# Another order of the head's stages, and q and k of nine head pairs in 2 KB rows

## The chip, the cores and the metric

The kernel runs on one core of one Trainium2 chip. The metric is the device time of one execution in microseconds (us), and the figure of a kernel is the median of its runs. One further execution of the kernel before was taken with the profiler; the profile and the trace are of that execution.

## The reference

Two attentions are computed over the same q, k and v (8 batches, 8 heads, 576 tokens, 64 values a head), and their sum goes through a gated feed-forward network.

```python
q_d, k_d, v_d = (t.reshape(B, H, 144, 4, D).mean(axis=3) for t in (q, k, v))
out_up = np.repeat(sm_attn(q_d, k_d, v_d), 4, axis=2)        # pooled: softmax over 144 means
mask = np.abs(pos[:, None] - pos[None, :]) < 4               # local: a band of 7 keys
out_local = softmax(where(mask, scale * q @ k.T, -1e9)) @ v
x = (out_up + out_local).transpose(0, 2, 1, 3).reshape(4608, 512)
out = (np.maximum(x @ w_gate, 0) * (x @ w_val)) @ w_out      # 512 -> 1536 -> 512
```

## The kernel before

The work comes in 32 pairs of heads. A pair is one round, `s`; four pairs make a batch. The instructions of each engine run in the order in which the program issues them; that order is written out by hand, and no scheduler changes it.

A round does the following for its pair. `load_qk` and `load_v` fetch q, k and v into the staging tiles `qst`, `kst` (four buffers each) and `vst` (three) by DMAs that SP issues. `cast_q`, `cast_k` (two halves, c = 0 and 1) and `cast_v` turn them into 16-bit tiles `qk16` and `vw`. For the first nine pairs (`N_PE = 9`) `turn_pe` transposes q and k on TensorE into `qkT` and sums groups of four tokens into `pd` with further matmuls; from pair 9 on `turn_dma` transposes by DMA and `pool_q` and `pool_k` make the sums on GpSimd.

`pooled_v` averages v; `scores` makes the scores of both attentions in the PSUM tile `at`, which all rounds share. The pooled branch is `pooled_max`, `pooled_exp` (two heads, four activations in all), `pooled_weights` (division by the sums) and `turn_pooled`, a DMA transpose that SP issues, or `turn_pooled_pe`, the same on TensorE. The local branch is `local_max`, `local_sub`, `local_exp`, `local_sum`, `local_weights` and `turn_local`, a transpose on VectorE. Two rounds later `pooled_out` and `local_out` make the two outputs, `evict_od` copies the pooled one out of PSUM, and `add_x` writes the sum into `xT`, the input of the network. `evict_vd` copies the averaged v out.

The network runs in units. A unit `h` makes 128 of the 1536 hidden values for 512 tokens: eight 128x512 matmuls (`h_ps`, L480), a relu on ScalarE (L489) and a product on VectorE (L490). A unit `y` makes 128 rows of the output in twelve matmuls (L495). There are 108 units `h` and 36 units `y`; `ffn(n)` issues the next n. The first 512 tokens are all of batch 0, so the first unit needs `add_x` of pairs 0 to 3.

The head is the code ahead of the loop over s = 4 to 33. It runs rounds 0 to 3 without units, then the outputs of pairs 2 and 3:

```python
for s in range(4):
    scores(s); pooled_v(s)
    if s >= 2:
        outputs(s - 2); evict_od(s - 2)
    cast_q(s + 1, "act"); cast_k(s + 1, 1, "pool")
    ...
    pooled_weights(s, True)        # four tensor_scalar on VectorE
    ...
    turn_local(s)
for p in (2, 3):
    outputs(p); evict_od(p); add_x(p)
```

In the loop a round issues up to four units (`early`: three in round 4, two in rounds 5 to 7, one in round 8, four from round 9 on). The weights are loaded by GpSimd's queue: `wg` and `wv` in six pieces of 256 columns each, three in the head and three in rounds 4 to 6, and `wo` in twelve pieces.

SP has one queue for all loads, the DMA transposes and the stores of the output. Its instructions go in order, so one that waits holds up those behind it.

In the kernel before, q of a pair is fetched as 96 x 12 rows of 256 B (token t in column t / 96 of partition t % 96), and k in 80 x 4 rows of 1 KB, four tokens each, with an overlap for the band's edges.

Of the kernel before, what the change touches and what calls it, by code (L numbers as in the profile page):

```python
# [16 lines left out]
N_PE = 9  # L17
# [3 lines left out]
def _np_constants():  # L21

    p = np.arange(128)
    g, i = p // 32, p % 32
    j = np.arange(32)
    diff = (j[None, :] - 4) - i[:, None]
    inside = np.abs(diff) <= 3
    mask = np.zeros((128, 6, 32), np.float32)
    for n in range(6):
        key = 24 * (4 * n + g)[:, None] - 4 + j[None, :]  # L30
        ok = inside & (key >= 0) & (key < 576)
        mask[:, n, :] = np.where(ok, 0.0, NEG)
    mask[i >= 24] = 0.0

    p32 = np.zeros((128, 32), np.float16)
    own = (i >= 4) & (i < 28)
    p32[p[own], (6 * g + (i - 4) // 4)[own]] = 0.25

    eye = np.zeros((96, 192), np.float16)
    eye[:, :96] = np.eye(96)  # L40
    eye[1:73, 96:168] = np.eye(72)
    eye[np.arange(96), 168 + np.arange(96) // 4] = 1.0
    return mask, p32, eye
# [17 lines left out]
def kernel(  # L61
# [39 lines left out]
    qst = many(4, [96, 2, 6, 64], FP32, "qst")  # L101
    kst = many(4, [96, 2, 2, 256], FP32, "kst")
# [3 lines left out]
    qk16 = many(2, [96, 14, 128], FP16, "qk16")  # L106
# [5 lines left out]
    eye = pool.tile([96, 192], FP16, name="eyec")  # L112
# [20 lines left out]
    def load_qk(p):  # L133
        base = 2 * p * S * D
        nc.sync.dma_start(qst[p % 4], _dap(q, base, [[D, 96], [S * D, 2], [96 * D, 6], [1, D]]))

        st = kst[p % 4].rearrange("p h c e -> p (h c) e")
        base -= 256
        a, z = (1 if p == 0 else 0), (3 if p == NP - 1 else 4)
        nc.sync.dma_start(  # L140
            st[0:80, a:z, :],
            _dap(k, base + 72 * 256 * a, [[256, 80], [72 * 256, z - a], [1, 256]]),
        )
        if p == 0:
            nc.sync.dma_start(st[1:81, 0, :], _dap(k, base + 256, [[256, 80], [1, 256]]))
        if p == NP - 1:
            for lo, n in ((0, 64), (57, 16)):
                nc.sync.dma_start(
                    st[lo : lo + n, 3, :],
                    _dap(k, base + (216 + lo) * 256, [[256, n], [1, 256]]),  # L150
                )
# [42 lines left out]
    def cast_q(p, eng):  # L194
        copy(
            eng,
            qk16[p % 2][:, 0:6, :].rearrange("p j (h d) -> p j h d", d=D),
            qst[p % 4].rearrange("p h j d -> p j h d"),
        )

    def cast_k(p, c, eng):
        copy(
            eng,
            qk16[p % 2][0:74, 6 + 4 * c : 10 + 4 * c, :].rearrange("p r (h d) -> p r h d", d=D),
            kst[p % 4][0:74, :, c, :].rearrange("p h (r d) -> p r h d", d=D),
        )
# [8 lines left out]
    def turn_pe(p):  # L215
        x16, xt, pdt = qk16[p % 2], qkT[p % 3], pd[p % 3]
        tq = fpsum.tile([128, 6, 96], FP16, name="tq_ps", tag="f")
        for j in range(6):
            nc.tensor.transpose(tq[:, j, :], x16[:, j, :], eye[:, 0:96])
        nc.scalar.copy(out=xt[:, 0:6, :], in_=tq)  # L220
        tk = fpsum.tile([128, 8, 80], FP16, name="tk_ps", tag="f")
        for j in range(8):
            nc.tensor.transpose(tk[:, j, :], x16[0:80, 6 + j, :], eye[0:80, 0:80])
        nc.vector.tensor_copy(out=xt[:, 6:14, 0:80], in_=tk)
        pq = fpsum.tile([128, 2 * SD], FP32, name="pool_ps", tag="f")
        for j in range(6):
            nc.tensor.matmul(
                out=pq[:, 24 * j : 24 * j + 24],
                lhsT=x16[:, j, :],
                rhs=eye[:, 168:192],  # L230
                start=True,
                stop=True,
            )
        for c in range(2):
            for r in range(4):
                nc.tensor.matmul(
                    out=pq[:, SD + 72 * c : SD + 72 * c + 72],
                    lhsT=x16[0:80, 6 + 4 * c + r, :],
                    rhs=eye[0:80, 96:168],
                    start=(r == 0),  # L240
                    stop=(r == 3),
                )
        nc.scalar.copy(out=pdt.rearrange("p t g -> p (t g)"), in_=pq)

    def turn_dma(p):
        nc.sync.dma_start(
            qkT[p % 3], qk16[p % 2].rearrange("p j f -> p (j f)"), transpose=True
        )
# [55 lines left out]
    def scores(p):  # L304
        qt = qkT[p % 3].rearrange("p j t -> p (j t)")
        kt, pdt = k_view(qkT[p % 3]), pd[p % 3]
        for c in range(2):
            for h in range(2):
                lo = 64 * h
                nc.tensor.matmul(  # L310
                    out=at[0:72, h, SCO + SD * c : SCO + SD * c + SD],
                    lhsT=pdt[lo : lo + 64, 0, 72 * c : 72 * c + 72],
                    rhs=pdt[lo : lo + 64, 1, :],
                    start=True,
                    stop=True,
                    tile_position=(lo, 0),
                )
        for n in range(6):
            for g in range(4):
                c, m = n // 3, 4 * (n % 3) + g  # L320
                for h in range(2):
                    lo = 64 * h
                    nc.tensor.matmul(  # L323
                        out=at[32 * g : 32 * g + 32, 2 + h, SCO + 32 * n : SCO + 32 * n + 32],
                        lhsT=qt[lo : lo + 64, 96 * n + 24 * g : 96 * n + 24 * g + 32],
                        rhs=kt[lo : lo + 64, c, :, 6 * m : 6 * m + 8].rearrange("p r g -> p g r"),
                        start=True,
                        stop=True,
                        tile_position=(lo, 32 * g),
                    )  # L330
# [73 lines left out]
    def pooled_weights(p, apart):  # L404
        c = col[p % 2]
        nc.vector.reciprocal(out=c[0:72, 48:52], in_=c[0:72, 44:48])
        if not apart:
            ed = e_d[p % 2][0:72].rearrange("p h c n j -> p (h c) n j")[:, :, 0:6, 0:24]
            nc.gpsimd.tensor_tensor(  # L409
                out=ed, in0=ed, in1=_sap(c, (0, 72), 48, [[1, 4], [0, 6], [0, 24]]), op=ALU.mult  # L410
            )
            return
        for hc in range(4):
            ed = e_d[p % 2][0:72, hc // 2, hc % 2, 0:6, 0:24]
            nc.vector.tensor_scalar(
                out=ed, in0=ed, scalar1=c[0:72, 48 + hc : 49 + hc], scalar2=None, op0=ALU.mult
            )
# [8 lines left out]
    def turn_pooled_pe(p):  # L426
        tp = fpsum.tile([128, 8, 72], FP16, name="ad_ps", tag="f")
        ed = e_d[p % 2].rearrange("p h c (k n) j -> p (h c k) (n j)", k=2)
        for j in range(8):
            nc.tensor.transpose(tp[:, j, :], ed[0:72, j, :], eye[0:72, 0:72])  # L430
# [107 lines left out]
    nc.vector.memset(kst[0][0:32, 0, 0, :], 0.0)  # L538
    nc.vector.memset(vst[0][0:32, 0, 0, :], 0.0)
    load_qk(0)  # L540
    load_qk(1)
    load_v(0)
    load_qk(2)
    load_v(1)
    load_qk(3)
    load_v(2)
    for t in qk16:
        nc.gpsimd.memset(t[64:96, 6:14, :], 0.0)
# [4 lines left out]


    def piece(i):
        load_w(moe_w_gate, wg, 256 * i, 256 * i + 256)
        load_w(moe_w_val, wv, 256 * i, 256 * i + 256)
# [4 lines left out]

    cast_q(0, "act")
# [3 lines left out]
    turn_pe(0)  # L567
    for s in range(4):
        scores(s)
        pooled_v(s)  # L570
        if s >= 2:
            outputs(s - 2)
            evict_od(s - 2)
        cast_q(s + 1, "act")
        cast_k(s + 1, 1, "pool")
        evict_vd(s, 0)
        pooled_max(s)
        pooled_exp(s, 0)
        cast_k(s + 1, 0, "dve")
        local_max(s)  # L580
        local_sub(s)
        turn_pe(s + 1)
        pooled_exp(s, 1)
        local_exp(s)
        evict_vd(s, 1)
        cast_v(s + 1, "pool")
        pooled_weights(s, True)
        if s < 2:
            turn_pooled(s)
        local_sum(s)  # L590
        local_weights(s)
        if s >= 2:
            add_x(s - 2)
            turn_pooled_pe(s)
        turn_local(s)
        if s == 0:
            load_v(3)
            load_qk(4)
        elif s == 1:
            load_v(4)  # L600
        else:
            load_qk(s + 3)
            piece(s - 2)
            load_v(s + 3)
    for p in (2, 3):
        outputs(p)
        evict_od(p)
        add_x(p)
    piece(2)
    cast_q(5, "act")  # L610
    cast_k(5, 0, "dve")
    cast_k(5, 1, "act")

    def weights(s, part):
        if s < 7 and part in (0, 2):
            src, dst = (moe_w_gate, wg) if part == 0 else (moe_w_val, wv)
            load_w(src, dst, 256 * (s - 1), 256 * s)
# [3 lines left out]
    early = {4: (1, 1, 1, 0), 5: (1, 1, 0, 0), 6: (1, 1, 0, 0), 7: (1, 1, 0, 0), 8: (1, 0, 0, 0)}  # L621
    for s in range(4, NP + 2):
# [37 lines left out]
        if now:  # L660
            local_exp(s)
            evict_vd(s, 1)
            pooled_weights(s, False)
# [10 lines left out]
        if nxt and s + 1 < N_PE:  # L674
            turn_pe(s + 1)
# [38 lines left out]
```

## Time and profile before

| | |
|---|---|
| runs | 406.16 us median of 3 (404.42 to 406.97) |
| profiled execution | 406.47 us, of which 404.7 us from the first to the last instruction (the span) |
| TensorE busy | 360.9 us, 89% of the span |
| VectorE, ScalarE, GpSimd busy | 222.5, 213.0 and 185.3 us |
| DMA packets | 164,887, of which 142,173 under 512 B; 60.47 MB |
| mean granted TensorE clock | 0.979 of full speed |

How to read it: PE is TensorE, PEld its weight loads, DVE VectorE, ACT ScalarE, POOL GpSimd, and SP SyncE; a q behind the name is the engine's queue. L323 is line 323 of the kernel before. In the view by slices each digit is the busy share of a fortieth of the span in tenths, 9 for 90% or more; PEclk is the granted clock in the same way, and DMA the mean busy share of 16 DMA engines. In the groups of instructions a row has line, engine, operation, what it writes and reads, shapes and count, then the busy time in all and the mean ns of one, then the idle time ahead of them and what ended it. The chain of waits is followed back from the last instruction, at each step to what released it.

A view by DMA window counts the packets that start in the window by size, cumulatively.

### The profile page before, as it was taken

The numbers are of one execution on the slowest core, as the hardware profiler recorded it, in microseconds if no ns is written. First come the engines' busy times: TensorE is split into PE (matmuls) and PEld (weight loads), VectorE is DVE, ScalarE is ACT, GpSimd is POOL, SyncE is SP. The second block draws the span as 40 slices with busy tenths as digits, with TensorE's granted clock in tenths as the row PEclk, the third lists the DMA queues.
The fourth block names the chain that finished last, engine by engine and source line by source line (L and its number), as shares of the span: only waits on it lengthen the run. The fifth ranks groups of instructions, "written<-read, shape, count | busy, mean of one in ns | idle before, by whom it ended". The sixth has DMA issues, their size and how long they took to land.

```text
span 404.7 us, 12822 instructions
## 1 busy us (share of the span) xinstructions
PE 360.9 (89%) x5276; PEld 183.3 (45%) x5276; DVE 222.5 (55%) x456; ACT 213.0 (53%) x608; POOL 185.3 (46%) x256
## 2 busy tenths in 40 slices
PE   2444499768989999999999999999999999999996
PEld 2333354434444444455554444444444444444442
DVE  1465667757566666666666666666656332222210
ACT  3444567655566665665566666666654332332321
POOL 4334655657766666666555556666574000000000
PEclk9999998966999999999999999999999999999999
DMA  9989999999999999989999999999731200100112
GB/s 176 201 157 201 205 117 223 181 207 175 205 212 184 199 207 188 190 182 200 192 183 189 182 210 194 192 184 163 144 79 47 67 28 26 52 28 26 43 44 96
DMA packets 164887, 60.47 MB, mean 149 GB/s; under 512 B 142173, under 2 KB 160221, under 8 KB 164829
## 3 DMA queue, kind: packets, MB, share of 16 engines
q1 hardware_dynamic: 156364, 54.79, 71.9%
q0 software_dynamic: 8064, 4.72, 9.0%
q8 instruction: 41, 0.67, 0.7%
q10 hardware_dynamic: 400, 0.14, 0.2%
q14 instruction: 18, 0.14, 0.1%
HBM read 42.08 MB, written 9.44 MB: 127 GB/s over the span
## 4 chain that ended last, share of the span: by engine, by line
PE 77%; DVE 4%; ACT 3%; DMA 2%; POOL 2%; issue 2%; POOLq 0%; DVEq 0%; ACTq 0%
PE h_ps L480 43%; PE y_ps L495 23%; PE at L336 4%; PE at L323 3%; DMA qkT<-qk 2%; PE at L310 2%; PE at L279 1%; PE at L294 1%; DVE xT L462 1%; DVE col L349 1%; ACT e_d L383 1%; ACT r L489 1%; DVE gT L490 0%; ACT qkT L220 0%; ACT qk L188 0%
## 5 line engine op out<-in xcount | busy, mean ns | idle before, releaser
L490 DVE TENSOR_TENSOR gT<-r,h_ps 128x512 f16<-128x512 f16 x108 | 73.1, 677 | 80.3 <-PE h_ps L480 60.8
L480 PE MATMUL h_ps<-xT,wv 128*128 128x512 f16 x432 | 114.2, 387 | 1.9 <-issue 1.4
L480 PE MATMUL h_ps<-xT,wg 128*128 128x512 f16 x432 | 114.8, 389 | 0.0
L495 PE MATMUL y_ps<-wo,gT 128*128 128x512 f16 x432 | 98.5, 379 | 1.0 <-ACT r L489 1.0
L489 ACT ACTIVATE r<-h_ps 128x512 f16<-128x512 f32 x108 | 64.4, 596 | 46.7 <-PE h_ps L480 46.7
L371 POOL TENSOR_TENSOR dd<-sm,col 128x384 f32<-128x384 f32 x32 | 26.6, 830 | 104.3 <-DVE col L368 104.3
L480 PEld LDWEIGHTS <-wv 128*128 128x128 f16 x432 | 43.1, 100 | 55.7 <-issue 6.8
L495 PEld LDWEIGHTS <-gT 128*128 128x128 f16 x432 | 42.3, 98 | 52.1 <-issue 1.3
L480 PEld LDWEIGHTS <-wg 128*128 128x128 f16 x432 | 40.5, 99 | 46.6 <-issue 3.6
L383 ACT ACTIVATE e_d<-at,col 72x144 f16<-72x144 f32 x128 | 46.5, 370 | 14.3 <-DVE sm L362 9.0
L349 DVE TENSOR_REDUCE col<-at 72x4 f32<-72x576 f32 x32 | 24.0, 750 | 33.7 <-ACT vd L397 33.7
L504 ACT COPY y_sb<-y_ps 128x512 f32<-128x512 f32 x36 | 20.9, 581 | 38.7 <-PE y_ps L495 38.7
L455 ACT CAST odx<-at 128x144 f16<-128x144 f32 x32 | 8.9, 278 | 59.1 <-PE at L336 58.1
L449 DVE STREAM_TRANSPOSE pT<-pp 128x384 f16<-128x384 f16 x32 | 18.5, 578 | 34.0 <-POOL pp L441 34.0
L409 POOL TENSOR_TENSOR e_d<-e_d,col 72x576 f16<-72x576 f16 x28 | 32.0, 1143 | 3.6 <-DMA qst<-in_q_dram 1.2
L192 POOL CAST vw<-vst 128x768 f16<-128x768 f32 x32 | 26.4, 824 | 6.7 <-DMA vst<-in_v_dram 6.7
L441 POOL TENSOR_TENSOR pp<-ee,col 128x384 f16<-128x384 f16 x32 | 26.5, 827 | 5.7 <-DVE col L438 5.7
L188 ACT CAST qk<-qst 96x768 f16<-96x768 f32 x32 | 26.7, 836 | 1.3 <-DMA qst<-in_q_dram 1.3
L462 DVE TENSOR_TENSOR xT<-at,odx 128x576 f16<-128x576 f32 x32 | 23.7, 742 | 2.6 <-ACT odx L455 1.8
L383 ACT ACTIVATION_READ_ACCUMULATOR e_d<-at,col 72x1 f32 x128 | 25.0, 196 | 0.0
L190 DVE CAST qk<-kst 74x512 f16<-74x512 f32 x33 | 20.2, 614 | 5.9 <-DMA kst<-in_k_dram 5.9
L252 POOL TENSOR_TENSOR ptq<-qkT 128x288 f32<-128x288 f16 x23 | 18.7, 814 | 3.1 <-DMA qkT<-qk 3.1
(52 smaller groups left out, 355.8 us busy)
## 6 DMA issues: line engine op xcount, KB each, us to landing
vst<-in_v_dram SPq DMA_DIRECT2D x126, 96.0 KB
kst<-in_k_dram SPq DMA_DIRECT2D x30, 320.0 KB
qst<-in_q_dram SPq DMA_DIRECT2D x32, 288.0 KB
out_dram<-y_sb SPq DMA_DIRECT2D x36, 256.0 KB
wg<-in_moe_w_gate_dram POOLq DMA_DIRECT2D x6, 256.0 KB, 5.9
wv<-in_moe_w_val_dram POOLq DMA_DIRECT2D x6, 256.0 KB, 6.2
wo<-in_moe_w_out_dram POOLq DMA_DIRECT2D x12, 128.0 KB, 6.1
kst<-in_k_dram SPq DMA_DIRECT2D x2, 240.0 KB
```

The lines of the kernel that those rows point to most:

```text
L188: nc.scalar.copy(out=out, in_=in_)
L192: nc.gpsimd.tensor_copy(out=out, in_=in_)
L349: nc.vector.tensor_reduce(out=c[0:72, 36:40].rearrange("p (h c) -> p h c", h=2), in_=at[0:72, 0:2, SCO : SCO + 2 * SD].rearrange("p h (c j ...
L371: nc.gpsimd.tensor_tensor(out=dd[p % 2], in0=sm[p % 2], in1=_sap(col[p % 2], (0, 128), 0, [[1, 12], [0, 32]]), op=ALU.subtract,)
L383: nc.scalar.activation(out=e_d[p % 2][0:72, h, cc, 0:6, 0:24], in_=at[0:72, h, lo : lo + SD].rearrange("p (n j) -> p n j", j=24), func=AF.Exp,
L409: nc.gpsimd.tensor_tensor(out=ed, in0=ed, in1=_sap(c, (0, 72), 48, [[1, 4], [0, 6], [0, 24]]), op=ALU.mult)
L441: nc.gpsimd.tensor_tensor(out=pp[p % 2], in0=ee[p % 2], in1=_sap(col[p % 2], (0, 128), 24, [[1, 12], [0, 32]]), op=ALU.mult,)
L462: nc.vector.tensor_tensor(out=xT[:, kk, b * S : (b + 1) * S].rearrange("p (n g m f) -> p g n m f", n=6, g=4, f=4), in0=at[:, :, U : U + SD ...
L480: nc.tensor.matmul(out=ps, lhsT=w[:, kk, 128 * j : 128 * j + 128], rhs=xT[:, kk, TCH * c : TCH * c + TCH], start=(kk == 0), stop=(kk == 3),)
L489: nc.scalar.activation(out=r, in_=h1, func=AF.Relu)
L490: nc.vector.tensor_tensor(out=gT[c % 2][:, j, :], in0=r, in1=h2, op=ALU.mult)
L495: nc.tensor.matmul(out=ps, lhsT=gT[c % 2][:, j, 128 * t : 128 * t + 128], rhs=wo[:, j, :], start=(j == 0), stop=(j == NJ - 1),)
```

## The change

The head has five rounds instead of four. In them:

- the order in a round is `pooled_v`, `pooled_out` of two rounds before, `scores`, `local_out`; `turn_local(s - 1)` comes behind `local_max(s)`;
- the casts are two pairs ahead of the round instead of one;
- `turn_pe` only issues the matmuls; the three copies out of PSUM are functions of their own (`evict_q`, `evict_k`, `evict_pooled`) with a place of their own in the order;
- `pooled_weights` is always the one instruction on GpSimd;
- the transpose of the pooled weights of pairs 0 and 1 by DMA is issued at the start of the next round, and that of pairs 2 and 3 on TensorE in the next round;
- the outputs of pair 3 come in round 4, and three units and the two transposes of pair 4 follow the last round;
- `wg` and `wv` come in pieces of 256, 256, 512 columns in the head, and 512 in round 5.

For the first nine pairs q and k are both loaded as 80 partitions x 2 heads x 512 values: a row of 2 KB holds eight tokens. Partition i of the first 72 holds tokens 8i to 8i + 7. `turn_pe` makes 8 + 8 transposes of 72 columns and 16 pooling matmuls of 72 columns (before: 6 of 96, 8 of 80, 6 of 24 and 8 of 72). The copies write every eighth column of `qkT` (`evict_q`, `evict_k`) and every second of `pd`.

The diff, cut to its core:

```diff
 def load_qk(p):
     base = 2 * p * S * D
+    if p < N_PE:
+        for src, dst in ((q, qst), (k, kst)):
+            nc.sync.dma_start(
+                dst[p % 4][0:80, :].rearrange("p (h e) -> p h e", h=2),
+                _dap(src, base, [[512, 80], [S * D, 2], [1, 512]]),
+            )
+        return
...
 def turn_pe(p):
+    x16 = qk16[p % 2][0:72]
...
     for j in range(8):
+        nc.tensor.transpose(tq[:, j, :], x16[:, j, :], eye)
+    for j in range(8):
+        nc.tensor.transpose(tk[:, j, :], x16[:, 8 + j, :], eye)
+    pq = fpsum.tile([128, 4, 72], FP32, name="pool_ps", tag="f")
+    for a in range(4):
+        for f in range(4):
             nc.tensor.matmul(
+                out=pq[:, a, :], lhsT=x16[:, 4 * a + f, :], rhs=eye,
+                start=(f == 0), stop=(f == 3),
+            )
+    return tq, tk, pq
+
+def evict_q(p, ps):
+    nc.scalar.copy(out=flat(p)[:, 0:S].rearrange("p (i u) -> p u i", u=8), in_=ps[0])
+
+def evict_k(p, ps):
+    nc.vector.tensor_copy(
+        out=flat(p)[:, S + 4 : 2 * S + 4].rearrange("p (i u) -> p u i", u=8), in_=ps[1]
+    )
+
+def evict_pooled(p, ps):
+    nc.scalar.copy(
+        out=pd[p % 3].rearrange("p t (i a) -> p t a i", a=2),
+        in_=ps[2].rearrange("p (t a) i -> p t a i", t=2),
+    )
...
-    for s in range(4):
+    for s in range(5):
+        if s in (1, 2):
+            turn_pooled(s - 1)
+        if s < 3:
+            load_v(s + 3)
+            load_qk(s + 4)
+        pooled_v(s)
+        if s >= 2:
+            pooled_out(s - 2)
+        scores(s)
+        if s >= 2:
+            local_out(s - 2)
+            evict_od(s - 2)
+        cast_v(s + 1, "pool")
+        evict_vd(s, 0)
+        pooled_max(s)
+        local_max(s)
+        local_sub(s)
+        if s >= 1:
+            turn_local(s - 1)
+        ps = turn_pe(s + 1)
+        evict_q(s + 1, ps)
+        pooled_exp(s, 0)
+        pooled_exp(s, 1)
+        evict_vd(s, 1)
+        evict_k(s + 1, ps)
+        evict_pooled(s + 1, ps)
+        if s >= 3:
+            turn_pooled_pe(s - 1)
+        cast_k(s + 2, 0, "dve")
+        cast_k(s + 2, 1, "pool")
+        pooled_weights(s)
+        if s >= 2:
+            add_x(s - 2)
+        if s == 4:
+            outputs(3)
+            evict_od(3)
+            add_x(3)
+        local_exp(s)
+        local_sum(s)
+        local_weights(s)
+        cast_q(s + 2, "act")
+        if s >= 3:
+            load_v(s + 3)
+        if s == 3:
+            load_qk(7)
+        if 1 <= s < 3:
+            piece(256 * (s - 1), 256 * s)
+        elif s == 3:
+            piece(512, 1024)
+    ffn(3)
+    turn_local(4)
+    turn_pooled(4)
```

## The prediction

> **What bounds the kernel now.** I read the page's slices first, then the chain of waits, then the rows by form of 26 to 46 us, then the DMA windows.
>
> ```profile
> PE   2444499768989999999999999999999999999996
> DVE  1465667757566666666666666666656332222210
> PEclk9999998966999999999999999999999999999999
> DMA  9989999999999999989999999999731200100112
> ```
>
> A slice is 10.1 us. From the eleventh on TensorE is full: there the chain of work holds h_ps and y_ps matmuls alone, and a round of four units repeats every 9.49 us. Nothing in the change reaches that stretch, so its worth is how much earlier the stretch begins. In the first five slices PE is half idle, and DMA is full.
>
> The chain of waits, in order of time (start, us, what), one head round and the outputs behind it:
>
> ```profile
> 39.09 0.76 DVE col L349
> 40.43 0.71 PE tk_ps L223 x8
> 42.12 0.84 ACT e_d L383 x4
> 43.19 1.25 DVE e_d L415 x4
> 44.43 0.47 DVE col L437
> 45.16 0.62 DVE xT L462
> 46.25 0.56 PE at L336 x40
> 47.14 0.77 DVE xT L462
> 49.28 0.77 DVE xT L462
> 51.39 4.87 PE h_ps L480 x16
> ```
>
> Short pieces on three engines hand over to each other; no piece waits for a load. In the timeline scores (L310) start at 9.51, 18.18, 25.61 and 35.78 us, the outputs of pair 2 at 45.82, the first h_ps at 51.32, pooled_v of round 5 at 58.95. A round with outputs takes 10.17 and 10.04 us.
>
> The durations, from the rows by form of 26 to 46 us (busy us, mean ns):
>
> ```profile
> L415 DVE TENSOR_SCALAR e_d<-e_d,col 72x144 f16<-72x144 f16 x9 | 2.7, 355 | 0.1
> L188 ACT CAST qk<-qst 96x768 f16<-96x768 f32 x2 | 1.7, 830 | 0.0
> L349 DVE TENSOR_REDUCE col<-at 72x4 f32<-72x576 f32 x2 | 1.5, 754 | 3.0 <-ACT vd L397 3.0
> L462 DVE TENSOR_TENSOR xT<-at,odx 128x576 f16<-128x576 f32 x2 | 1.4, 694 | 0.0
> L220 ACT COPY qkT<-tq_ps 128x576 f16<-128x576 f16 x2 | 1.2, 624 | 0.0
> L224 DVE COPY qkT<-tk_ps 128x640 f16<-128x640 f16 x2 | 1.0, 480 | 0.0
> L243 ACT CAST pd<-pool_ps 128x288 f16<-128x288 f32 x2 | 0.8, 398 | 0.7 <-PE pool_ps L236 0.7
> ```
>
> DMA packets in three windows: 12 to 18 us, 81.5 to 82.6 us, 20.2 to 24.2 us:
>
> ```profile
> DMA packets 3366, 1.23 MB, mean 205 GB/s; under 512 B 2872, under 2 KB 3365, under 8 KB 3365
> DMA packets 471, 0.29 MB, mean 267 GB/s; under 512 B 240, under 2 KB 471, under 8 KB 471
> DMA packets 2805, 0.69 MB, mean 173 GB/s; under 512 B 2805, under 2 KB 2805, under 8 KB 2805
> ```
>
> The last is q, v and transposes alone: 4 us of 16 engines at 97% over 2805 packets is 22 ns for one of 256 B. The other two then give 66 and 53 ns for a k packet of 1 KB. So today q costs 1152 x 22 / 16 = 1.6 us of all engines, k (320 packets) 1.06 to 1.32, v (1536) 2.1, the e_d transpose (640) 0.9.
>
> **The change part by part.** *Loads.* q and k of nine pairs become 160 packets of 2 KB each, 320 KB on 80 partitions. No row shows such a load. Lower bound: the best quarter-microsecond slices between 40 and 50 us show 356 GB/s, hence 0.92 us; upper: k at 1.32 us for the same bytes on the same partitions. I take 1.1, near k's cheaper window. A pair then needs 2.2 + 2.1 = 4.3 us instead of about 4.9.
>
> The Trainium skill ("SBUF — State Buffer", Door 1: The DMA port swizzle) says that DMA speed hangs on how many of 16 ports the partitions reach; partitions 0 to 63 share eight of them. By its 435 GB/s the 64 x 4 KB would take an estimated 1.2 us however long the rows are, which adds 1.0 us to the sum; the 1.06 us window is a little better than the rule, the 1.32 us one agrees.
>
> *Start.* In the order of the changed program the ACT table load (1.28 us, at 2.12 now) stands behind the wait for pair 0's q. With that landing near 4.2: table load, cast of 1024 elements (0.83 and 0.61 us for 768 and 512 give 1.05), transposes 1.28, pooling matmuls 1.28 (16 x 72 columns; 8 x 72 take 0.64), pd 0.40: scores near 9.6, as now.
>
> *Rounds 0 and 1.* pooled_exp no longer waits between casts, the normalising leaves DVE (four L415) for POOL (1.14 us, L409), turn_local moves behind the next maximum. By the same rows these two rounds need 5.2 us each, so compute could start round 2 at 20. But pooled_out(0) now stands in PE ahead of scores(2), and waits for the e_d transpose of pair 0, which in SP's one queue stands behind q, k of pairs 0 to 4 and v of 0 to 3. Supply: first packet 1.8 + constants 0.5 + 10 x 1.1 + 4 x 2.1 + 0.9 = 22.6 us, then pooled_out 0.43: scores(2) at 23.1 against 25.6. Bounds by the load's price: 21.3 and 25.3. Behind that PE wait stands every scores and transpose of round 2, and ACT and DVE wait for those.
>
> *Rounds 2 to 4.* PE's block (pooled_v, scores, both outputs) keeps its length, 2.06 us from 35.78 to 37.84. Then odx 0.28 and vd 0.26 on ACT, and on DVE maximum 0.75 + 0.17, mask 0.56, row maximum 0.55, turn_local 0.58, evict_k, cast 0.42, reciprocal 0.17, add_x 0.69. evict_k writes every eighth element; nothing in the trace does that. Lower: 0.43 (L224 by its elements), upper: 0.76 (the slower L462); I take 0.6. With 0.2 for four handovers a round is 2.06 + 0.54 + 4.49 + 0.2 = 7.3 us. Hidden under it: ACT's 5.5 us (exponentials 1.45, evict_q 0.62, adT 0.64, cast 1.05 and the small ones) and POOL's 5.8 (casts, subtraction, two products, two weight issues). DMA is just even: a round calls for 2.1 (v), 2.2 (q, k) and two weight pieces, 7.3 us in all (q0's 9.0% of 404.7 us over 24 issues is 1.5 each); with loads at 1.32 us it is 0.4 a round short, less what was fetched ahead. evict_q strided like evict_k has 1.24 as its upper bound (POOL's 2.16 ns an element in L371, the slowest row); it has 1.48 us of cover, maximum and mask.
>
> The Trainium skill ("VectorE: DVE Perf Modes", What auto-detection actually checks) grants the doubled 16-bit rate only with a step of one. By it evict_k falls to an estimated 0.73 us, and the three rounds grow by 0.4 us in all; L224's 0.48 us for 640 elements shows that it has the doubled rate now.
>
> *Outputs of pair 3, units.* Round 4 ends with pooled_out and local_out of pair 3, 1.03 us, in place of the 5.5 us from 45.82 to 51.32. The first h_ps starts at 23.1 + 3 x 7.3 - 0.83 + 1.03 = 45.2, against 51.32: 6.1 us earlier. Pair 4 is done by then, so three units follow without the 1.05 us of transposes at 56.1: 6.8 us instead of 7.6. Round 5 starts at 52.0, 6.9 us earlier.
>
> *Rounds 5 to 8.* These last 6.75, 8.72, 8.73 and 9.9 us on a chain through ACT. Two of its casts of q grow by 0.22, three transposes by 0.1, three evict_k by 0.12; evict_q between 0 and 0.62 each. On the path at most 3.0 us, at least 0; I take 0.7. Weights: the same bytes in twelve DMAs fall to eight, hidden, since column 1024 is first read in round 7. SP's transpose of pair 4 still stands ahead of pair 8's loads, whose first cast is in round 6.
>
> *Rounds 9 and 10* take 11.1 and 11.2 us instead of 9.49. In one of them POOL waits for qkT:
>
> ```profile
> 93.05 8.79 DMA qkT<-qk
> ```
>
> Less queued load can give back 0 to 3.3 us. Loads from pair 9 on are unchanged, so I take 0.
>
> Sum: -6.9 + 0.7 = -6.2 us. The profiled execution took 406.47 us (span 404.7, 1.8 around it), 0.3 above the median of the runs; so 400.3 on its scale, 400.0 against the median of 406.16.
>
> **The rivals.**
>
> *A. Supply binds the whole head (slower).* If a 2 KB load costs 1.8 us, scores(2) start at 30.1 and each later round needs 2.1 + 3.6 + 3.0 = 8.7 us of DMA instead of 7.3; the first h_ps comes at 56.4, the end at 411.2. It breaks even near 1.5 us, slower by over 1% from 1.75. For it: DMA is full throughout the head. Against: 1.32 us is the worst k window.
>
> *B. The clock.* PEclk falls to 0.55 from 83.7 to 93.6 us, and h_ps at L480 costs 1.9 us for four there instead of 1.03. With one more such stretch over two of rounds 5 to 8, two units cost 3.5 us and the pair's own work 1.0 more, less 1.7 of idle PE: +2.8 a round, 405.6. For: PE has gaps there. Against: three dense units now precede round 5.
>
> *C. Rounds 9 and 10 become plain.* Half to all of the 3.3 us: 396.7 to 398.4. For: the line above; against: supply there is of the old form.
>
> *D. The gain is taken back by later transfers.* If supply sets round 9, only the saved load time counts: nine pairs at 0.6 = 5.4 us, less the 0.7, or as little as 3: 401.5 to 403.5. For: DMA slices stay at 9; against: 54.5 to 60 us has idle DMA that the new order can fill.
>
> **How the numbers follow.** Forecast 0.58 (its own range 397.5 to 402.5), A 0.07, B 0.13, C 0.11, D 0.11. A measurement of this kernel tells about 1% from no change, 402.1 and 410.2. Below 402.1: nearly all of the forecast (0.55), C, half of D: 0.72. Slower by over 1%: A, 0.07. Within: 0.21. The range runs from most of C to B, 395.5 to 405.6.
>
> **What would show it.** Right: scores of rounds 2 to 5 at about 23, 30, 38 and 52; pooled_out(0) waiting for a DMA; two round steps near 7.3; first h_ps near 45; 9.49 us rounds afterwards. Wrong: a round over 8.5 (then evict_k or the loads); scores(2) after 26 (rival A); rounds 5 to 8 over 36 us in all against 34.1 (B, or the strided evictions). A first h_ps before 46 with an end after 402 would mean D.

## The result and the profile after

The kernel after takes 410.83 us (median of 4 runs, 410.69 to 411.72); the kernel before took 406.04 beside it (4 runs). The ratio is 1.0127, with an interval of 1.0091 to 1.0163: slower by 1.3%, where 400.0 was forecast. The profiled execution took 410.69 us, with a span of 408.9.

The slices show the same full TensorE from the eleventh on, and the same full DMA ahead of it. In the clock row four slices are below 9, the eighth to the eleventh; before it were three:

```profile
PE   2635467776999999999999999999999999999996
PEclk9999999886899999999999999999999999999999
DMA  8999997999999999999999999998641200010012
```

Two rows of the groups of instructions (line, shapes and count, then busy us and mean ns of one) stand out against L220 and L224 of before, 624 and 480 ns:

```profile
L263 ACT COPY qkT<-tq_ps 128x576 f16<-128x576 f16 x9 | 24.5, 2723 | 2.0 <-PE tq_ps L244 1.7
L266 DVE COPY qkT<-tk_ps 128x576 f16<-128x576 f16 x9 | 24.3, 2695 | 1.6 <-PE tk_ps L246 1.6
```

`evict_q` and `evict_k` each cost 2.7 us, nine times. The chain of waits in order of time (start, us, what) has one of them in every round from 2 to 7, and in front of them one wait for a DMA. (Two more, 2.17 and 2.68 us, stand on it at 8.01 and 12.70 us, ahead of this cut.)

```profile
20.97 6.44 DMA adT<-e_d
27.41 0.04 issue
27.45 0.43 PE at L325 x6
...
32.33 2.59 DVE qkT L266
...
41.48 2.59 DVE qkT L266
...
50.64 2.59 DVE qkT L266
...
55.21 4.93 PE h_ps L510 x16
...
67.86 2.63 ACT qkT L263
...
78.50 2.62 ACT qkT L263
...
89.02 2.62 ACT qkT L263
```

The transpose of pair 0's pooled weights is issued at 20.97 us and has landed 6.4 us later; only then can `pooled_out(0)` and the scores of round 2 behind it start.

The steps beside their forecast, from the timelines of after and of e6, the experiment that takes both causes away:

| | before | forecast | after | e6 |
|---|---|---|---|---|
| scores(2) | 25.61 | 23.1 | 27.81 | 22.44 |
| rounds 2, 3, 4 (from scores on; round 4 to the first h_ps) | 10.17, 10.04 | 7.3, 7.3, 7.5 | 8.84, 9.02, 9.48 | 7.92, 8.94, 8.22 |
| first h_ps | 51.32 | 45.2 | 55.15 | 47.52 |
| `pooled_v` of round 5 | 58.95 | 52.0 | 61.80 | 54.14 |
| rounds 5 to 8 in all, from scores to scores | 34.0 | 34.8 | 38.0 | 32.4 |
| rounds 9 and 10 in all | 22.5 | 22.3 | 20.6 | 20.6 |

From round 11 on a round takes 9.44 to 9.54 us in all of them.

### The profile page after: what moved, and what is told of

It is laid out like the page before. It is cut to its first block, busy times and chain, and to the rows that moved or that the text cites. A ratio compares the mean times of both kernels' runs of the same rounds, so it can differ in the third digit from the quotient of the medians.

```text
span 408.9 us, 12885 instructions
## 1 busy us (share of the span) xinstructions
PE 361.5 (88%) x5312; PEld 184.7 (45%) x5312; DVE 237.6 (58%) x445; ACT 230.9 (56%) x606; POOL 188.0 (46%) x258
## 3 DMA queue, kind: packets, MB, share of 16 engines
HBM read 42.35 MB, written 9.44 MB: 127 GB/s over the span
## 4 chain that ended last, share of the span: by engine, by line
PE 82%; DVE 7%; ACT 7%; DMA 3%; POOL 1%; issue 1%; ACTq 0%; DVEq 0%; POOLq 0%
PE h_ps L510 46%; PE y_ps L525 23%; PE at L373 4%; PE at L360 4%; ACT qkT L263 3%; PE at L340 2%; DVE qkT L266 2%; DMA adT<-e_d 2%; PE at L310 1%; PE at L325 1%; DVE col L386 1%; DMA qst<-in_q_dram 1%; ACT qk L192 1%; DVE xT L492 1%; DVE col L405 1%; DVE sm L399 1%
## 5 line engine op out<-in xcount | busy, mean ns | idle before, releaser
L420 ACT ACTIVATE e_d<-at,col 72x144 f16<-72x144 f32 x128 | 47.7, 380 | 6.8 <-DVE sm L399 6.8
L445 POOL TENSOR_TENSOR e_d<-e_d,col 72x576 f16<-72x576 f16 x32 | 36.6, 1144 | 11.5 <-issue 4.0
L192 ACT CAST qk<-qst 96x768 f16<-96x768 f32 (+1 forms) x32 | 28.7, 896 | 0.0
L471 POOL TENSOR_TENSOR pp<-ee,col 128x384 f16<-128x384 f16 x32 | 26.5, 828 | 2.8 <-DVE col L468 2.8
L310 PE MATMUL at<-vw,p32c 128*32 128x128 f16 (+1 forms) x256 | 10.0, 222 | 17.9 <-DVE xT L492 9.1
L263 ACT COPY qkT<-tq_ps 128x576 f16<-128x576 f16 x9 | 24.5, 2723 | 2.0 <-PE tq_ps L244 1.7
L194 DVE CAST qk<-kst 74x512 f16<-74x512 f32 (+1 forms) x33 | 22.1, 672 | 5.4 <-DMA kst<-in_k_dram 5.4
L266 DVE COPY qkT<-tk_ps 128x576 f16<-128x576 f16 x9 | 24.3, 2695 | 1.6 <-PE tk_ps L246 1.6
```

Of the source, the lines that this page charges most:

```text
L192: nc.scalar.copy(out=out, in_=in_)
L263: nc.scalar.copy(out=flat(p)[:, 0:S].rearrange("p (i u) -> p u i", u=8), in_=ps[0])
L266: nc.vector.tensor_copy(out=flat(p)[:, S + 4 : 2 * S + 4].rearrange("p (i u) -> p u i", u=8), in_=ps[1])
L420: nc.scalar.activation(out=e_d[p % 2][0:72, h, cc, 0:6, 0:24], in_=at[0:72, h, lo : lo + SD].rearrange("p (n j) -> p n j", j=24), func=AF.Exp,
L445: nc.gpsimd.tensor_tensor(out=ed, in0=ed, in1=_sap(c, (0, 72), 48, [[1, 4], [0, 6], [0, 24]]), op=ALU.mult)
L471: nc.gpsimd.tensor_tensor(out=pp[p % 2], in0=ee[p % 2], in1=_sap(col[p % 2], (0, 128), 24, [[1, 12], [0, 32]]), op=ALU.mult,)
```

## The experiments

The theory: the two evictions at a step of eight elements are the loss. The rivals: the supply of the head by DMA, and the new order itself.

**e1: the same reordering, on the side that reads PSUM.**

```diff
-        out=flat(p)[:, 0:S].rearrange("p (i u) -> p u i", u=8), in_=ps[0]
+        out=flat(p)[:, 0:S].rearrange("p (i u) -> p i u", u=8),
+        in_=ps[0].rearrange("p u i -> p i u")
```

(`evict_k` likewise.)

> The kernel after with one edit: evict_q and evict_k write qkT contiguously and do the reordering on the side that reads PSUM (step of 72 elements between neighbours). Theory (the two evictions' writes at a step of 16 bytes, 2.7 us each instead of 0.62 and 0.48, are the loss): each falls to 0.6 to 0.9 us, scores(2) come about 1.5 us earlier (near 26.3), the rounds 2 to 4 take about 7.3 us instead of 8.8 to 9.0, first h_ps near 48 instead of 55.15, rounds 5 to 8 about 6 us shorter; 398 to 401 us. Rival supply (the head waits for loads and for the pooled transpose behind them, the evictions are only filler): evictions fall, the head does not, first h_ps stays at 54 to 55, only rounds 5 to 7 gain; about 405. Rival order (the new order of stages is what loses): 408 to 411, with the head's round steps unchanged. Rival either side (a step of 72 elements on the reading side costs as much as the writes did): evictions stay near 2.7 us and the time near 410.8.

Measured 406.67 us, 1.0003 of before (0.9977 to 1.0029). The evictions fell to 637 and 736 ns:

```profile
L263 ACT COPY qkT<-tq_ps 128x576 f16<-128x576 f16 x9 | 5.7, 637 | 2.3 <-PE tq_ps L244 1.9
L269 DVE COPY qkT<-tk_ps 128x576 f16<-128x576 f16 x9 | 6.6, 736 | 1.4 <-PE tk_ps L246 1.4
```

But scores(2) came at 28.15, scores(3) at 36.85, and the first h_ps at 52.05. Only the step from round 3 to round 4, 7.16 us, was as forecast, and the time is above the theory's 398 to 401. TensorE stands still from 22.06 to 27.79 us ahead of `pooled_out(0)`, and the chain of waits names what holds round 3 now:

```profile
27.63 8.81 DMA adT<-e_d
36.45 0.04 issue
36.49 0.43 PE at L329 x8
```

So the evictions are a cause, and a second one stands behind them: the pooled transposes. That of pair 1 takes 8.8 us from issue to landing. In the kernel after the long evictions hide that wait.

**e3: the order alone**, with the loads, casts, transposes and contiguous evictions of the kernel before.

> The order of stages of the kernel after with the loads, casts, transposes and contiguous evictions of the kernel before. Theory (strided evictions are the loss, the order is a gain): evict_q 0.62, evict_k 0.48, rounds 2 to 4 near 7.3 us, first h_ps 46 to 49 us, time 399 to 403 us. Rival order: no better than before, 406 us or more, with rounds of 8.5 us or more although the evictions are short. Rival supply: the pair's loads are 0.3 to 0.5 us longer than with 2 KB rows, scores(2) come at 27 us or later and the rounds at 8 us or more; 404 to 408.

Measured 405.75 us, 0.9986 (0.9966 to 1.0007). scores(2) at 27.21, then steps of 8.5, 6.6 and 9.6 us, first h_ps at 51.95. The order alone changes the time by no more than the interval allows, and it meets the same wait for a transpose (the waits of TensorE up to 125 us: us in total, times, longest):

```profile
PE at L302 <- DMA adT<-e_d: 6.0, 3, 3.6
```

So the 2 KB rows do not make that wait. The last step has a pause of TensorE of 2.40 us and round 7 one of 3.31 us for which no wait is shown; the last section comes back to such pauses.

**e4: the rows alone**, the 2 KB loads with strided evictions in the order of before; later the same with contiguous evictions (**e4 read**).

> The order of stages of the kernel before with the 2 KB loads, the casts, transposes and strided evictions of the kernel after. Theory: each of the nine turns puts 2.0 to 2.2 us more on the chain, in the head five times (pair 0 and rounds 0 to 3) and in rounds 4 to 7 on ScalarE; 406 + 9 x 2.1 = 425 at most, 414 at least if half is hidden. Rival order: the rows are a gain and the order is the loss, so this one is faster than before, 400 to 404. Rival supply: evictions hidden, the time is that of before, 404 to 408.

> The order of stages of the kernel before with 2 KB loads and the turns of the kernel after, but contiguous evictions (as e1). Beside e4, which had the strided ones and took 415.5, it gives their price in the old order, and beside the kernel before the worth of the rows alone. Theory (rows are a small gain, 0.1 to 0.2 us a pair of DMA, and the larger casts and turns cost about as much): 404 to 407, 9 to 11 less than e4. Rival (rows are worth the 4 us that e6 and e12 show): 401 to 403.

Measured 415.54 us (ratio 1.022, 1.0184 to 1.0256) and 405.29 (0.9974, 0.9949 to 1.0). In the old order the strided evictions cost 10.2 us, and the rows by themselves are worth 0.3%, by the interval between nothing and 0.5%.

**e5: the copies and the loads by themselves.** Groups of four copies of 128x576 values, one kind a line, output zeros:

```python
for _ in range(4): nc.scalar.copy(out=d8.rearrange("p (i u) -> p i u", u=8)[:, :, 0], in_=src)
```

> No attention and no network: the output is zeros; groups of four copies of 128x576 16-bit values and groups of four loads, by themselves. Theory (the step of the writes sets the price, on either engine and alone): ScalarE 0.62 us and VectorE 0.5 us at step 1; about 2.7 us at step 8 on both, whether in rows of 72 or in one row of 576, and whether from PSUM or from SBUF; step 16 no cheaper than step 8; steps 2 and 4 between; reading PSUM at a step of 72 elements with contiguous writes 0.6 to 0.9 us. Rival contention (the two engines disturb each other): 0.6 to 0.8 us alone and 2.7 us only where both write at the same time. Rival rows (eight short rows cost, not the step): step 8 in one row of 576 near 0.6 us. Loads: 2 KB rows 0.92 to 1.1 us each alone, 1 KB rows 1.06 to 1.32, 256 B rows 1.6; a 2 KB load between 256 B loads 1.4 us if mixing costs, 1.0 if not.

From the groups of instructions by form: ScalarE at a step of 1, 4 and 8 values (L110, L114, L116); reading PSUM at a step of 72 and writing contiguously (L126); VectorE at 1 and 8 (L133, L139), the read-side form (L149); GpSimd at 8 from SBUF (L155); ScalarE at 8 while VectorE does the same (L158):

```profile
L110 ACT COPY d<-src 128x576 f16<-128x576 f16 x4 | 2.5, 637 | 0.1
L114 ACT COPY d<-src 128x576 f16<-128x576 f16 x4 | 5.7, 1432 | 0.1
L116 ACT COPY d<-src 128x576 f16<-128x576 f16 x4 | 10.9, 2728 | 0.1
L126 ACT COPY o<-src 128x576 f16<-128x576 f16 x4 | 2.6, 639 | 0.1
L133 DVE COPY d<-src 128x576 f16<-128x576 f16 x4 | 1.8, 455 | 0.1
L139 DVE COPY d<-src 128x576 f16<-128x576 f16 x4 | 10.8, 2711 | 0.1
L149 DVE COPY o<-src 128x576 f16<-128x576 f16 x4 | 3.0, 758 | 0.1
L155 POOL COPY o<-x 128x576 f16<-128x576 f16 x4 | 10.9, 2726 | 131.2 <-DVE o L153 131.0
L158 ACT COPY o<-src 128x576 f16<-128x576 f16 x4 | 10.8, 2702 | 74.5 <-DVE d L156 74.5
```

For copies out of PSUM the step of the writes sets the price, on ScalarE and VectorE, alone or together, in one row of 576 or in eight of 72 (2.70 to 2.71 us). GpSimd was measured at a step of 8 alone. The source matters on VectorE: from SBUF the same copy takes 1.44 us. A step of 2 costs 0.80 us on ScalarE and 0.79 on VectorE, 16 no more than 8 (2.65 and 2.61). Contention and short rows are out. Reading PSUM at a step of 144 bytes costs ScalarE nothing, and VectorE 0.30 us.

The loads alone, in the middle of their groups, ran at 256 GB/s with 2 KB rows, 247 with 1 KB rows and 209 with 256 B rows of v; that is 1.28, 1.33 and 1.41 us for a load of 320, 320 and 288 KB. 2 KB and 256 B loads in turn ran at 218. Doubling the rows from 1 to 2 KB saves k 0.05 us.

**e10: loads by partitions.**

> Loads only, in groups of eight of one kind, output zeros: 256 KB on 64 partitions as 2 x 2 KB rows each, on 128 partitions as one 2 KB row each, on 64 and on 128 partitions in 256 B rows, then 320 KB on 80 partitions in 2 KB rows and in 1 KB rows. Theory partitions (the price of these loads is set by how many partitions they reach, not by their rows): 80 partitions cost 1.36 us a load in either row length (240 GB/s), 64 partitions about 1.2 us for 256 KB (220 GB/s) and 128 partitions 0.7 to 0.8 (330 GB/s or more) with 2 KB rows; with 256 B rows both 1.3 to 1.5 us. Rival rows (row length sets it): 64 and 128 partitions alike with 2 KB rows, near 1.1 us. Rival memory side (the source limits the rate to 240 GB/s at any layout): 1.1 us for each 256 KB.

The DMA view over the middle of three groups: 64, 128 and 80 partitions (the other three, of the same partitions in the other row length, ran at 200, 317 and 239 GB/s).

```profile
DMA packets 382, 1.25 MB, mean 208 GB/s; under 512 B 78, under 2 KB 78, under 8 KB 382
DMA packets 747, 1.36 MB, mean 340 GB/s; under 512 B 84, under 2 KB 84, under 8 KB 747
DMA packets 491, 1.69 MB, mean 241 GB/s; under 512 B 80, under 2 KB 80, under 8 KB 490
```

That is 1.26 us for 256 KB on 64 partitions, 0.77 on 128, and 1.36 for 320 KB on 80. In this kernel the rows of one partition lie behind one another in memory and travel as packets of up to 4 KB whatever their nominal length, so it says nothing on rows; e5 does. From 64 to 128 partitions the rate rises 1.6 times, as the Trainium skill has it ("SBUF — State Buffer", Door 1: The DMA port swizzle): it gives 196 GB/s for partitions 0 to 63 and 328 for all 128.

**e6: the pooled transposes of pairs 0 and 1 on TensorE too**, on top of e1.

```diff
-        if s in (1, 2):
-            turn_pooled(s - 1)
...
-        if s >= 3:
+        if s >= 1:
             turn_pooled_pe(s - 1)
```

> The kernel e1 (contiguous evictions) with the pooled transposes of pairs 0 and 1 made on TensorE, one round later, as those of pairs 2 and 3 are, instead of by SP's DMA. Theory supply (DMA throughput as a whole holds the head; the transposes only stand at its end): scores(2) come at 25 to 27 us, when v of pair 2 and its cast are there, the first h_ps 3 to 4 us earlier than 52.1, and rounds 8 to 10 give most of it back since the loads and transposes of pair 9 and 10 come when DMA is through: 404 to 406 us. Rival queue (the transposes' place in SP's queue is the whole delay): scores(2) near 22, first h_ps near 45, time 399 to 401. Rival nothing: 406 to 407, first h_ps near 52.

Measured 399.22 us, 0.9841 (0.9801 to 0.9881): faster than both kernels by 1.6 and 2.8%, and within 0.8 us of the forecast. The theory of supply expected 404 to 406 and fell; the rival "queue" held in its time and in scores(2), 22.44, but its first h_ps near 45 came at 47.52. The chain of waits has no DMA transfer between 16.1 and 83.5 us:

```profile
21.54 0.50 ACT adT L465
22.04 0.04 issue
22.08 0.43 PE at L329 x7
...
31.63 1.62 issue
...
47.59 6.62 PE h_ps L514 x24
```

Two pauses of TensorE for which no wait is shown lie on it, 1.62 us in round 3 and 0.43 in round 4. The trace of e13 below, whose program is the same up to round 8, has none there and its first h_ps at 45.95; so 1.6 us of the head of e6 are no part of the change.

**e8 and e9: loads taken away**, from e1 (e8) and from the kernel after (e9): q and k of pairs 4 to 8 and v of pairs 3 to 8.

> The kernel e1 without the loads of q and k of pairs 4 to 8 and of v of pairs 3 to 8: the rounds use the data of earlier pairs that lie in the buffers, so the output is not the reference's; all compute stays. Theory supply: scores(2) at 21 to 23 us instead of 28.4, rounds of 7.2 us, first h_ps at 43 to 46 instead of 52.1, the e_d transposes land within 4 us of their issue, rounds 9 and 10 near 9.5 us instead of 11: 388 to 395 us. Rival head only (supply holds the head, not rounds 8 to 10): 397 to 400. Rival chain (compute and handovers hold the head): first h_ps within 2 us of 52, 403 to 407.

> The kernel after, strided evictions and all, with the same loads left out as in e8. It gives the price of the strided evictions where loads do not cover them. Theory: 2.1 us in each of round 0, rounds 2 to 4 and rounds 5 to 7 are on the path, so 10 to 15 us more than e8, where the difference of the kernel after to e1 is 4.4. Rival (the evictions are never worth more than 4 to 5 us, other work covers the rest): 3 to 6 us more than e8.

Measured 400.05 (0.985, 0.9817 to 0.9883) and 407.83 us (1.0054, 1.0029 to 1.008). In e8 scores(2) come at 22.72 and the first h_ps at 45.6. But an estimated 24 us of DMA time gone (ten loads at 1.28 us, and six of v, 384 KB each, at the 209 GB/s of e5) bring no more than the two transposes moved in e6, not the 388 to 395 of the theory, and rounds 8 to 10 stay about as long (7.9, 10.6 and 10.5 us). The profiled execution of e8 has a pause of 3.1 us in round 7, so its time says little on small differences. The heads say more: without pauses in either, the first h_ps comes at 45.6 with the loads gone and at 45.95 with them there and the transposes on TensorE (e13). So the loads that e8 leaves out hold the head mainly by way of the transposes. With no more than the rest of one pair's loads ahead of it, one still takes 3.9 us to land:

```profile
18.41 3.90 DMA adT<-e_d
```

The strided evictions cost 7.8 us here, less than the 10 to 15 expected, and nearer to them in the profiled executions (9.7): 1.0 ahead of the first scores, 2.0, 1.5 and 1.5 in rounds 2 to 4, 2.0 and 3.0 in rounds 5 and 6, nothing in rounds 0 and 1, and 1.3 less in round 7, where e8 has that pause and e9 none.

**e11: the transposes cured, the strided evictions kept.**

> The kernel after with its strided evictions, and the pooled transposes of pairs 0 and 1 on TensorE as in e6. Theory two overlapping causes (the wait for the transposes and the long evictions partly cover each other; where the transposes are gone, the evictions cost the 7.8 us that e9 and e8 show): first h_ps near 52, time 406 to 408. Rival additive (the transposes cost their 7.2 us whatever the evictions take): 403 to 404. Rival evictions cover all of the wait: 409 to 411.

Measured 408.59 us (1.0066, 1.0039 to 1.0093); first h_ps at 51.84, close to the theory of two overlapping causes. With it the square is complete (us):

| | transposes by DMA | on TensorE |
|---|---|---|
| evictions strided | 410.8 (after) | 408.6 (e11) |
| evictions contiguous | 406.7 (e1) | 399.2 (e6) |

Either cure alone brings 2.2 or 4.2 us; both bring 11.6. The two waits lie beside each other in rounds 2 and 3, so each covers part of the other. The sizes are rough: the profiled executions of e1 and e6 have pauses without a wait on their chains (2.57 us in round 7 of e1, 2.05 in the head of e6), those of after and e11 none over a microsecond up to 120 us.

**e12: order and transposes with the old loads.**

> The order of stages of the kernel after with the loads, casts and turns of the kernel before (as e3), and the pooled transposes of pairs 0 and 1 on TensorE. Theory (row length is worth next to nothing, since e5 and e10 price a load by its partitions: 1.36 us against 1.5 for q and 1.35 for k): within 2 us of e6, 397 to 401. Rival rows (the 2 KB loads are needed for the gain): 402 to 405.

Measured 403.15 us (0.9941, 0.9922 to 0.996): 3.9 us more than e6, against the expectation and inside the range of the rival "rows". The profile puts most of it in one place. scores(2) come at 24.50 instead of 22.44, where k of pair 2 lands at 17.5 instead of 16.1, but the first h_ps makes that good (47.19 against 47.52). Round 7 takes 12.4 us instead of 8.6, with a pause of TensorE for which no wait is shown:

```profile
70.92 3.38 issue
```

Round 10 takes 11.2 instead of 10.0. So what the rows are worth is open: 3.9 us here with that pause, 0.3% in e4, and between e3 and e1, which differ in the rows and what hangs on them, nothing clear of the intervals (405.75 and 406.67).

**e7: fewer weights in the head**: columns 768 to 1024 come in round 5 instead of 3, the last 512 in round 6 instead of 5. **e13: one unit more in round 8** (`early[8]` (1, 1, 0, 0)). **e14: `add_x(s - 2)` ahead of `evict_k` and the cast of k** in the head. All on top of e6.

> The kernel e6 with one quarter less of the gate and value weights in the head: columns 512 to 768 in round 3, 768 to 1024 in round 5, the last 512 in round 6. Theory (with the transposes on TensorE the head is a chain of short pieces and no longer waits for supply): 398 to 400.5, no difference. Rival supply: first h_ps up to 2 us earlier and 396 to 397.5. Rival late weights (units of rounds 6 and 7 wait for their columns): 401 or more.

> The kernel e6 with two units in round 8 instead of one. Theory (TensorE idles 5 us of round 8, waiting for the pooled sums of pair 9 on GpSimd behind a load of v): a unit of 2.1 us fits into it, and the end comes 1.5 to 2.4 us earlier: 396.5 to 398. Rival (the unit's relu and product delay the chain on ScalarE and VectorE by as much): 398.5 to 400.

> The kernel e6 with add_x of two rounds before moved ahead of evict_k and the cast of k on VectorE, in rounds 2 to 4. Theory (VectorE's chain of short pieces sets these rounds, and the cast of k, 0.68 us, then runs beside the next round's matmuls): the three round steps each fall by 0.5 to 0.7 us, first h_ps 1.5 to 2 us earlier, 397 to 398. Rival (the end is set later, by supply in rounds 5 to 10): 398.5 to 400 although the first h_ps comes earlier. Rival (evict_k comes later and scores wait for it): no earlier first h_ps, 399 to 401.

e7: 405.94 us (1.0017, 0.9982 to 1.0051), as the rival of the late weights has it. The head is no faster (first scores of round 5 at 54.00 against 54.36 in e6 and 52.91 in e13), and the last weights come late: the chain has 13.2 us of waiting for `wv` from 68.8 on, and rounds 6 and 7 take 11.0 and 14.7 us.

e13: 419.18 us (1.033, 1.0294 to 1.0366). Both expectations failed. Every unit now stands one place earlier against the rounds, and in the full stretch one round in four takes 11.9 us or more: the first unit that needs the last pair of a batch is issued ahead of that pair's `add_x`. The waits of TensorE from 125 to 300 us (us in total, times, longest) show it; e6 has none there:

```profile
PE h_ps L514 <- DVE xT L496: 9.1, 4, 2.3
```

The other rounds take 9.85 us instead of 9.45, some 6 us of the 20 in all; why is open.

e14: 399.62 us (0.9824, 0.9761 to 0.9887), the same as e6. Rounds 2 to 4 take 6.9, 7.2 and 7.9 us, the first h_ps comes at 44.92 and `pooled_v` of round 5 at 51.52, on the forecast. That is 2.6 us earlier than in e6, but only 1.0 earlier than in e13, which has the order of e6 without its pauses (7.8, 7.65 and 8.0 us): the move of `add_x` is worth about 1.0 us here, the rest is the missing pauses. The gain is gone by round 9. The table by stage of e14 for rounds 6 and 7, and of e6 for the same two (stretch, length, busy us of PE, PEld, DVE, ACT, POOL with counts, granted clock, DMA):

```profile
58.80:69.00 10.20, 8.27 (x166) 4.53 (x164) 6.32 (x14) 6.00 (x18) 4.37 (x6) 0.83 1.38 148
69.00:79.40 10.40, 8.23 (x177) 4.47 (x177) 6.35 (x14) 5.78 (x18) 5.42 (x8) 0.84 1.30 183
```

```profile
61.40:69.40 8.00, 6.37 (x168) 4.04 (x164) 6.51 (x14) 6.11 (x18) 4.31 (x6) 1.00 1.23 195
69.40:78.00 8.60, 8.07 (x168) 4.34 (x164) 6.37 (x14) 5.90 (x18) 5.24 (x8) 0.80 1.27 192
```

The granted clock was 0.83 and 0.84 in the profiled execution of e14, which at 402.04 us is the longest of its four runs; the others took 397.53, 398.17 and 401.07. The clock is not the whole of it: e6 had 0.80 in round 7 and was 1.8 us shorter there. In e14 rounds 6 and 7 also have pauses without a wait, 1.20 and 1.39 us, and round 8, 11.9 us instead of 9.0, a wait of 3.42 us for a transpose that in e6 was 0.62. What brings these on, and whether the faster executions have them, is not shown.

## Why the prediction was wrong

The forecast was missed by 10.8 us, 10.4 in the profiled execution. Against the forecast's steps the kernel after loses 4.7 us up to scores(2), 5.2 in rounds 2 to 4 and 3.2 in rounds 5 to 8; it gains 1.7 in rounds 9 and 10 and about 1 elsewhere.

**The steps that failed.**

- *evict_k.* Taken at 0.6 us with an upper bound of 0.76 from L462; it measured 2.70, four and a half times as much, in three head rounds. The bound was wrong in kind: L462 writes runs of 24 values in one piece, so it shows nothing of a step of 16 bytes, and the far row at hand, 2.16 ns an element on GpSimd, was taken as the ceiling for `evict_q` alone. It was too low as well: 4.7 ns an element is what ScalarE and VectorE take out of PSUM, and GpSimd from SBUF.
- *evict_q.* Growth of 0 to 0.62 us; it was 2.1. In the head it is longer than its cover of 1.48 us, and in rounds 5 to 7 it lies on the chain with nothing beside it: rounds 5 to 8 took 38.0 us, over the 36 that the prediction named as a sign of its being wrong.
- *The transposes of pairs 0 and 1.* Placed rightly, behind the loads in SP's queue and ahead of every score of round 2, but priced at 0.9 us, their share of DMA time. That of pair 0 was forecast to land at 22.6; it was issued at 20.97, not late, and landed at 27.41 (8.8 us after issue for pair 1 in e1). The DMA packets by window take the 6.4 us apart, by an estimate from their sizes: packets of 2 KB, those of the loads ahead, run until about 24.4 us instead of the forecast's 21.7, and the transpose itself takes the 3.0 us from there on, of which DMA is almost idle for one (40 GB/s from 25.4 to 26.5). In e8 the loads ahead end near 19.6 us and the transpose takes 2.7 more. So issue to landing was the price, not the packets' time. This wait was put down once, for pair 0; pair 1 has it too (e1).
- *The load's price.* 1.1 us, with bounds of 0.92 and 1.32. Alone it is 1.28 to 1.36, no better than a k load in 1 KB rows (1.33). The rule of the Trainium skill that was set against it ("SBUF — State Buffer", Door 1: The DMA port swizzle), an estimate of 1.2 us at any row length, was nearer than the term. Ten loads at 1.3 instead of 1.1 us are 2.0 of the 2.7 us by which the loads ahead of the transpose were late; the rest is open. The loads do not make the miss by themselves: e6 has the same ones and scores(2) at 22.44.
- *Rounds 0 and 1.* Taken at 5.2 us each, with compute ready for round 2 at 20; in e6, where neither cause holds them, they take 5.95 and 6.56, and round 2's `pooled_out` starts at 22.08. That e6 meets scores(2) near the forecast's 23.1 is luck: there no DMA transpose stands ahead of it, and the chain runs from k of pair 2, landed at 16.14, through the short pieces of round 1.
- *Two readings* were a little off: from scores to scores round 8 of before lasts 9.76 us, not 9.9, and rounds 9 and 10 take 11.25 and 11.24.

**The steps that held.** The head's chain of short pieces, nearly: with both causes cured and no pauses the order as forecast (e13's head) has rounds of 7.8, 7.65 and 8.0 us for 7.3, 7.3 and 7.5 and the first h_ps at 45.95 for 45.2; with `add_x` moved (e14) 6.9, 7.2 and 7.9, and 44.9. Three units from 55.15 to 61.80, 6.65 us for 6.8. The full stretch at 9.44 to 9.54 us a round. So the head is worth about what was forecast, but only where `qkT` is written contiguously and the pooled transposes don't go by DMA. That e6 ends within 0.8 us of 400.0 is in part luck: its first h_ps is 2.3 us late, and rounds 5 to 8 are 2.4 and rounds 9 and 10 1.7 us shorter than forecast. Before had pauses of 1.43 and 1.71 us in rounds 7 and 8 that e6 hasn't.

**The rivals.** A (slower, 411.2) has the sign and the time, but not the mechanism: alone, 2 KB loads cost 1.28 to 1.36 us, not 1.8, and taking them away is worth no more than taking two transposes off the queue. C came half true: rounds 9 and 10 gave back 1.9 of the 3.3 us that it named at most. B shows in the kernel after as clocks of 0.84, 0.83 and 0.71 in rounds 6 to 8, but e6 has 0.80 and 0.86 in rounds 7 and 8 and reaches 399. D (401.5 to 403.5) was not met by any kernel that has the new rows and order; e12 lies there with the old loads.

The second rule that the prediction weighed, the Trainium skill's "VectorE: DVE Perf Modes", What auto-detection actually checks, gave 0.73 us for `evict_k`. In the form of e1, where only the reading side steps, it measured 0.736: the rule holds, but it speaks of the rate of processing, and the write at a step costs far more than the loss of the doubled rate.

## What to carry to other kernels

When a layout is turned on its way out of PSUM, put the step on the side that reads PSUM and write SBUF contiguously; out of PSUM a step of eight 16-bit values in the write makes the copy four to six times as long (e5). Price a DMA that something waits for by its time from issue to landing in the trace, not by the share of DMA time of its packets. Where two waits lie beside each other, curing one shows little: cure both in one kernel before a theory is dropped.

## What the runs showed of the hardware that was not expected

- The price of a write by its step (e5, 576 values of 16 bits out of PSUM): 0.64, 0.80, 1.43, 2.73 and 2.65 us on ScalarE at 2, 4, 8, 16 and 32 bytes; VectorE nearly the same but for 0.46 at 2 bytes. With 32-bit values a step of 16 bytes costs 1.17 and 1.16 us, against 0.72 and 0.80 at 4 bytes. From SBUF instead of PSUM VectorE needs 1.44 us at 16 bytes, ScalarE 2.73. The Trainium skill ("SBUF — State Buffer", Door 1: The DMA port swizzle, on cachelines of 16 bytes) says that 16-bit values can be strided by up to eight without cost; the measured writes differ: four to six times the cost at eight, and some already at two.
- A transpose of the pooled weights by DMA takes an estimated 2.7 to 3.0 us once the packets ahead of it are through (e8 and after), with DMA almost idle for part of it; its packets alone were priced at 0.9.
- Pauses of TensorE of 1.0 to 3.4 us for which no wait is shown ("issue" in the chain) stand beside packets of 16 KB of the instruction queue. In e12 the pause runs from 70.92 to 74.30 us and such a packet from 71.62 to 72.92; in e1 75.92 to 78.49 and 75.72 to 76.96; in the kernel before 77.39 to 78.82 and 75.89 to 77.22. That instructions come late behind the loads is what this suggests; no run tested it, and most such packets stand beside no pause: the kernel after has 41 of them and no pause over a microsecond in its first 120 us, and e13 has none in the head where e6, with the same program there, has 1.62 us.
